# Attention statistics moved from VectorE to GpSimd, with a re-ranked order of issue and a second output tile

## The chip, the core and the metric

The kernel runs on one core of a Trainium2 chip. TensorE (PE) multiplies matrices, VectorE (DVE), ScalarE (ACT) and GpSimd (POOL) work on tiles in SBUF, SyncE (SP) issues the transfers. Each engine takes its instructions in the order in which the program lists them and waits for the others by semaphores. The metric is the device time of one execution in microseconds (us), as the median of several runs.

## What is computed

The reference has three stages, each feeding the next. The inputs q and k are scaled by 8 in this case, so that the scores are far from zero and the maxima matter.

```python
q_pool = q.reshape(B, H, S // 2, 2, D).mean(axis=3)          # B 2, H 8, S 1152, D 64
scores = scale * np.matmul(q_pool, k.transpose(0, 1, 3, 2))
scores = scores - np.max(scores, axis=-1, keepdims=True)
attn = np.exp(scores)
attn = attn / (np.sum(attn, axis=-1, keepdims=True) + 1e-09)
x = np.matmul(attn, v)                                        # then (1152 tokens, 512)
out += p[:, e:e + 1] * (np.maximum(x @ w1[e], 0.0) @ w2[e])   # 4 experts, 1024 wide
y = elu(x @ w_in) @ w_out                                     # 2048 wide
```

## The kernel before

**Tiling.** There are 16 heads (2 batches of 8). Two heads make a pair; a pair has 1152 pooled queries, that is 9 blocks of 128 rows. The fifth block belongs half to the even head and half to the odd one. So there are 72 blocks, and 8 of them have the score matmuls of two heads. The 1152 keys of a block are cut in two parts, z = 0 (640 keys) and z = 1 (512 keys), each with a maximum and an exponential of its own.

**The steps of the attention, by their letters in the code.** S are the score matmuls of a block and part (`scores`, line 430). R is the negated maximum of the part on VectorE (`max_all`, line 450), E the exponential with its sum on ScalarE (`exp`, line 457). T transposes the exponentials, three 128x128 pieces at a time, into one of two PSUM banks (line 493); D and G copy such a bank into `pt` on VectorE or ScalarE (`evac`, line 500). V multiplies `pt` with v (`values`, line 513, two halves h), O copies the result from the same two banks into `xo` (line 539). Because the two parts were scaled by different maxima, each half of a head's result has to be multiplied by a factor. These factors come from the **statistics** of the head, tiles named `st` of 128 x 5 x 2 or 128 x 4 x 2 numbers: `st00`/`st10` hold the negated maxima of both parts, `st01`/`st11` the sums, `st02`/`st12` the factors. I (`greater`, line 473) takes the smaller negated maximum and the two differences, J (line 479) their exponentials on ScalarE, K (`factors`, line 483) the weighted sum, its reciprocal and the two factors. Steps 3 and 4 send the factors through DRAM and back, broadcast, as the tile `fb`. X (`x_scaled`, line 556, GpSimd) multiplies `xo` with `fb` and adds the two halves, H and L (lines 561 and 564) split the result in a high and a low part `XH`, `XL` for the next stage.

**Preparation of a head.** a, b, c make Q (sum of neighbours, high part, low part), d and e make the high and low part of K (`k_high` line 411 on ScalarE, `k_low` line 415 on GpSimd in two halves). q, k and v are the loads.

**What sets the order.** `order_of` (line 159) is a list scheduler that runs while the program is built. It has a table `STAGES` (line 27) with a cost for each step on each engine that may take it, and a rank offset; of the steps that could start first it takes the one of the lowest rank (block number plus offset). What it writes is the order on every engine's queue and, for D, G and O, the engine. Nothing is reordered on the chip.

**After the attention** come 12 groups of two weight matrices (`first` line 698, `second` line 720), three matmuls for each product with high and low parts (`product`, line 680). GpSimd makes the low part of the weights (`conv_low`, line 304).

Of the kernel before, what the change touches and what calls it, by code (L numbers as in the profile page):

```python
# [10 lines left out]
F32 = mybir.dt.float32  # L11
# [14 lines left out]

STAGES = {
    "S": (dict(PE=585), 8),
    "R": (dict(DVE=822), 1.5),
    "E": (dict(ACT=920), 4),  # L30
    "I": (dict(DVE=330), 2),
    "J": (dict(ACT=250), 1.5),
    "K": (dict(DVE=720), -8),
    "3": (dict(SP=500), 2),
    "4": (dict(SP=500), 2),
    "X": (dict(POOL=4240), 0),
    "T": (dict(PE=327), 2),
    "D": (dict(ACT=480, DVE=557), -4),
    "G": (dict(ACT=480, DVE=557), 0),
    "V": (dict(PE=2620), 6),  # L40
    "O": (dict(ACT=720, DVE=750), 0),
    "H": (dict(ACT=690), 8),
    "L": (dict(POOL=1414), 1),
    "a": (dict(POOL=1400), 5),
    "b": (dict(ACT=686), -2),
    "c": (dict(DVE=1400), 0.5),
    "d": (dict(ACT=1160), -3),
    "e": (dict(POOL=1450), 5),
    "q": (dict(SP=1900), -9),
    "k": (dict(SP=1900), -9),  # L50
# [22 lines left out]
MB = 9  # L73
# [6 lines left out]
def blocks_of(i):  # L80

    return range(MB * (i // 2) + 4 * (i % 2), MB * (i // 2) + 5 + 4 * (i % 2))


def attention_ops(NH, KC):

    ops = {}

    def op(rank, before, x, *k, after=0):
        ops[(x, *k)] = [b for b in before if b], rank + STAGES[x][1], after  # L90

    NB = NH // 2 * MB
    U = range(3)
    
    t = 2700
    for i in range(NH):
        b = blocks_of(i)[0]
        zs = range(2) if i < 2 else range(1)
        if i > 1:
            old = [(x, i - 2, z) for x in "be" for z in range(2) if (x, i - 2, z) in ops]  # L100
            old += [("c", i - 2, z) for z in range(2) if ("c", i - 2, z) in ops]
            op(b, old, "q", i)
            op(b, old, "k", i)
        op(b, [("V", i - 3, 1)] if i > 2 else [], "v", i, after=9000)

        free = [("S", x, z) for x in blocks_of(i - 4) for z in (0, 1)] if i > 3 else []
        for z in zs:
            t += 1700 if i < 2 else 0
            op(b, [i > 1 and ("q", i)], "a", i, z, after=t if i < 2 else 0)
            op(b, [("a", i, z), *free], "b", i, z)  # L110
            op(b, [("b", i, z)], "c", i, z)
            op(b, [i > 1 and ("k", i), *free], "d", i, z, after=t if i < 2 else 0)
        for z in range(2):
            op(b, [("d", i, z % len(zs))], "e", i, z)
    for b in range(NB):
        p, m = divmod(b, MB)

        hs = [2 * p] * (m < 5) + [2 * p + 1] * (m > 3)
        need = [(x, i, z) for x in "ce" for i in hs for z in range(2) if (x, i, z) in ops]
        if b < 2:  # L120
            need.remove(("c", 0, 1))
        for z in (0, 1):
            op(b + 0.3 * z, need, "S", b, z)
            op(b + 0.3 * z, [("S", b, z)], "R", b, z)
            op(b + 0.3 * z, [("R", b, z), *[("T", b - NP, u) for u in U if b >= NP]], "E", b, z)
        for u in U:
            op(b, [("E", b, z) for z in (0, 1) if (z == 0 and 3 * u < CUT) or (z and 3 * u + 3 > CUT)] + [("V", i - 2, 1) for i in hs if i > 1], "T", b, u)
            op(b, [("T", b, u)], "D", b, u)
            if m == 4:
                op(b, [("T", b, u)], "G", b, u)  # L130
        if m in (4, 8):
            i = hs[0]
            for h in (0, 1):
                cs = range(CUT, KC) if h else range(CUT)
                ds = [("D", x, u) for x in blocks_of(i) for u in sorted({c // 3 for c in cs})]
                if i % 2:
                    ds = [("G", *x[1:]) if x[1] == blocks_of(i)[0] else x for x in ds]
                op(b + 0.5 * h, ds + [("V", i, 0) if h else ("v", i)], "V", i, h)
                op(b + 0.5 * h, [("V", i, h)] + [("L", i - 2)] * (i > 1), "O", i, h)
            op(b, [("E", b, 0), ("E", b, 1)], "I", i)  # L140
            op(b, [("I", i)], "J", i)
            op(b, [("J", i)], "K", i)
            op(b, [("K", i), i > 1 and ("4", i - 2)], "3", i)
            op(b, [("3", i), i % 2 and ("3", i - 1), i > 1 and ("X", i - 2)], "4", i)
            op(b, [("O", i, 0), ("O", i, 1), ("4", i)], "X", i)
            op(b, [("X", i)], "H", i)
            op(b, [("H", i)], "L", i)
    op(0, [], "p", after=40000)
    w = NB - 30
    for j in range(8):  # L150
        op(w + j, [("S", w + j, 0)], "w", j)
# [78 lines left out]
def attention_then_moe_then_elu_ffn(  # L230
# [32 lines left out]
    XH = const.tile([P, DC, T], F32R, name="XH")  # L263
    XL = const.tile([P, DC, T], F32R, name="XL")
# [4 lines left out]
    def f(ap):  # L269
        return ap.bitcast(F32)  # L270
# [45 lines left out]
    with ExitStack() as actx:  # L316
# [4 lines left out]
        mx_p = actx.enter_context(tc.tile_pool(name="mx", bufs=1))  # L321
        x_p = actx.enter_context(tc.tile_pool(name="xp", bufs=1))
# [6 lines left out]
        HQ = Q // 2  # L329
# [48 lines left out]
        def half(z):  # L378
            return slice(z * HQ, z * HQ + HQ)
# [89 lines left out]
        def stats(i):  # L469
            c = slice(MH + 1, MB) if i % 2 else slice(0, MH + 1)  # L470
            return [t[:, c] for t in st[i // 2 % 2]]

        def greater(e, i):
            m, _, t = stats(i)
            tt("DVE", t[:, :, 0], m[:, :, 0], m[:, :, 1], ALU.min)
            tt("DVE", t[:, :, 1], t[:, :, 0], m[:, :, 1], ALU.subtract)
            tt("DVE", t[:, :, 0], t[:, :, 0], m[:, :, 0], ALU.subtract)

        def factors_exp(e, i):
            t = stats(i)[2]  # L480
            nc.scalar.activation(t, t, AF.Exp)

        def factors(e, i):
            m, s, t = stats(i)
            tt("DVE", s, s, t, ALU.mult)
            nc.vector.scalar_tensor_tensor(
                out=s[:, :, 0], in0=s[:, :, 0], scalar=1e-9, in1=s[:, :, 1], op0=ALU.add, op1=ALU.add
            )
            nc.vector.reciprocal(out=s[:, :, 0], in_=s[:, :, 0])
            for z in (0, 1):  # L490
                tt("DVE", t[:, :, z], t[:, :, z], s[:, :, 0], ALU.mult)

        def transposes(e, b, u, n):
            tb[b, u] = t = bank[n]
# [33 lines left out]
        def rows(i):  # L528
            return slice(D * (i % 2), D * (i % 2) + D)

        def x_part(i, t):
            b, h = heads[i]
            return t[rows(i), h // 2, b * Q : b * Q + Q]


        xo = x_p.tile([P, 2, Q], F32, name="xo")
        fb = x_p.tile([P, 2 * Q], F32, name="fb")

        def output(e, i, h):
            o = tb.pop((i, h))  # L540
            for z in (0, 1):
                copy(e, xo[rows(i), h, half(z)], o[D * z : D * z + D, :HQ])

        def factors_out(e, i):
            p, y = divmod(i, 2)
# [8 lines left out]
            nc.sync.dma_start(out=fb[rows(i)], in_=d.unsqueeze(0).to_broadcast([D, 2 * Q]))  # L554

        def x_scaled(e, i):
            x = xo[rows(i)]
            tt(e, x, x, fb[rows(i)].rearrange("p (q z) -> p z q", z=2), ALU.mult)
            tt(e, x[:, 0], x[:, 0], x[:, 1], ALU.add)

        def x_high(e, i):
            copy(e, x_part(i, XH), xo[rows(i), 0])

        def x_low(e, i):
            tt(e, x_part(i, XL), xo[rows(i), 0], f(x_part(i, XH)), ALU.subtract)

        def norm_probs(e):
            r = mx_p.tile([P, TC, E], F32, tag="pn", name="pn", bufs=1)
# [11 lines left out]
            nc.sync.dma_start(out=pr.rearrange("e (p c) -> p e c", p=P), in_=r)  # L580

        do = dict(
            S=scores, R=max_all, E=exp, I=greater, J=factors_exp, K=factors, X=x_scaled, T=transposes, V=values, O=output,
            H=x_high, L=x_low, q=load_q, k=load_k, v=load_v, a=q_sum, b=q_high, c=q_low,
            d=k_high, e=k_low, p=norm_probs, y=lambda e: load_w(1), w=lambda e, j: wops[j](),
            g=lambda e, j: conv_high(e, 0, j, w_e), f=lambda e, j: conv_low(e, 0, j),
            G=lambda e, b, u: evac(e, b, u, 1),
            D=lambda e, b, u: evac(e, b, u, 0 if b % MB == MH else None),
# [250 lines left out]
```

## Time and profile before

| | us |
|---|---|
| median of 3 runs | 910.0 (909.78 to 911.85) |
| the profiled execution | 911.97 |
| its span, first to last instruction | 910.3 |
| of it, up to the end of the last V | 304.8 |

The profile page gives the busy time of each engine, its share of the span, the costliest groups of instructions with what ended the idle time before them, and the chain of waits that ended last, followed back from the last instruction. PE is busy 95% of the span, VectorE 58%, ScalarE 40% and GpSimd 49%. These shares mix two stages that look different: the attention, where all four engines work on each other's results, and the two products behind it, where PE has no gap.

### The profile page before, as it was taken

The page shows a single profiled execution, that of the slowest core. Times are in us where ns is not written, and L with a number is a line of the kernel's source. Part 1 is how long each engine was busy: PE and PEld are TensorE (multiplying, and loading weights), DVE is VectorE, ACT ScalarE, POOL GpSimd, SP SyncE. Part 2 cuts the span into 40 slices and gives each one's busy share as a digit, 9 for nine tenths or more (in the row PEclk, how much of TensorE's full clock was granted, in tenths as well). Part 3 has the DMA queues.
Part 4 walks back from the last instruction along what each step waited for, and adds up shares of the span by engine and source line. Part 5 has one row for each costly group of instructions (what it writes and reads, how often), then busy time and mean ns, then how long its engine had stood idle before and what let it go on. Part 6 is the DMA issues. An engine that isn't in the chain of part 4 may idle for free.

```text
span 910.3 us, 13830 instructions
## 1 busy us (share of the span) xinstructions
PE 865.5 (95%) x5374; PEld 797.8 (88%) x5374; DVE 530.1 (58%) x820; ACT 366.6 (40%) x746; POOL 443.6 (49%) x298
## 2 busy tenths in 40 slices
PE   8898899787998999999999999999999999999998
PEld 7565667666676799999999999999999999999998
DVE  7897978878677145556465565465565632333333
ACT  5786867666676422221221221312213253313221
POOL 3366655564613632546555454546464472624321
PEclk9999999897999999999999999999999999999999
DMA  7466253651220243513343324324144211000011
GB/s 236 80 144 143 68 144 67 151 143 27 86 40 10 57 185 105 166 46 123 109 142 102 130 82 129 130 62 168 36 130 148 101 62 47 1 1 2 1 40 66
DMA packets 40353, 84.37 MB, mean 93 GB/s; under 512 B 14304, under 2 KB 17376, under 8 KB 37344
## 3 DMA queue, kind: packets, MB, share of 16 engines
q1 hardware_dynamic: 40288, 83.49, 32.1%
q8 instruction: 42, 0.69, 0.3%
q14 instruction: 23, 0.19, 0.1%
HBM read 72.63 MB, written 10.84 MB: 92 GB/s over the span
## 4 chain that ended last, share of the span: by engine, by line
PE 79%; DVE 11%; issue 3%; ACT 2%; POOL 2%; DMA 1%; SPq 0%; DVEq 0%; ACTq 0%; POOLq 0%
PE p L684 60%; PE t L519 8%; PE s L442 6%; PE t L496 5%; DVE st L278 4%; DVE st L453 3%; DVE pt L275 2%; POOL acc L739 1%; ACT e L459 1%; ACT pt L275 1%; DMA k<-in 1%; POOL l L278 1%; DVE xo L275 1%; POOL xo L278 0%; DVE nt L643 0%
## 5 line engine op out<-in xcount | busy, mean ns | idle before, releaser
L684 PE MATMUL p<-XH,h 128*128 128x384 f32 (+1 forms) x608 | 198.6, 327 | 2.4 <-DVE hl L706 2.0
L684 PE MATMUL p<-XL,h 128*128 128x384 f32 (+1 forms) x608 | 198.3, 326 | 0.0
L684 PE MATMUL p<-hh,l 128*128 128x384 f32 (+1 forms) x608 | 198.0, 326 | 0.2 <-POOL l L278 0.2
L684 PE MATMUL p<-XH,l 128*128 128x384 f32 (+1 forms) x608 | 198.2, 326 | 0.0
L684 PE MATMUL p<-hl,h 128*128 128x384 f32 (+1 forms) x608 | 197.9, 326 | 0.0
L684 PE MATMUL p<-hh,h 128*128 128x384 f32 (+1 forms) x608 | 197.9, 326 | 0.0
L278 POOL TENSOR_TENSOR l<-w,h 128x512 fp32r<-128x512 f32 x96 | 125.6, 1326 | 70.9 <-ACT h L275 70.8
L705 ACT ACTIVATE hh<-p 128x768 fp32r<-128x768 f32 (+1 forms) x50 | 39.4, 789 | 278.0 <-PE p L684 277.9
L706 DVE SCALAR_TENSOR_TENSOR hl<-p,hh 128x768 fp32r<-128x768 f32 (+1 forms) x50 | 46.3, 926 | 162.3 <-ACT hh L705 162.3
L496 PE MATMUL t<-ident,e 128*128 128x128 f32 x648 | 106.1, 289 | 32.4 <-DVE pt L275 24.3
L496 PEld LDWEIGHTS t<-ident,e 128*128 128x128 f32 x648 | 79.5, 146 | 59.1 <-DVE pt L275 31.6
L442 PE MATMUL s<-K,Q 128*128 128x320 f32 (+1 forms) x480 | 120.2, 372 | 4.2 <-DVE K L278 2.3
L684 PEld LDWEIGHTS p<-XH,h 128*128 128x128 f32 x608 | 114.1, 188 | 2.9 <-DVE hl L706 2.2
L684 PEld LDWEIGHTS p<-XL,h 128*128 128x128 f32 x608 | 114.1, 188 | 0.4 <-issue 0.4
L684 PEld LDWEIGHTS p<-hh,l 128*128 128x128 f32 x608 | 114.1, 188 | 0.4 <-POOL l L278 0.4
L684 PEld LDWEIGHTS p<-hh,h 128*128 128x128 f32 x608 | 114.1, 188 | 0.0
L684 PEld LDWEIGHTS p<-hl,h 128*128 128x128 f32 x608 | 114.1, 188 | 0.0
L684 PEld LDWEIGHTS p<-XH,l 128*128 128x128 f32 x608 | 114.1, 188 | 0.0
L453 DVE TENSOR_REDUCE st<-s 128x1 f32<-128x640 f32 (+1 forms) x144 | 104.9, 749 | 8.7 <-PE s L442 7.7
L459 ACT ACTIVATE e<-s,st 128x640 f32<-128x640 f32 (+1 forms) x144 | 106.4, 747 | 7.9 <-DVE st L453 7.5
L658 POOL TENSOR_TENSOR nt<-nt,ne 128x512 f32<-128x512 f32 x32 | 41.8, 1307 | 121.8 <-issue 61.5
L718 POOL TENSOR_TENSOR hl<-e,hh 128x768 fp32r<-128x768 f32 (+1 forms) x26 | 44.8, 1723 | 110.2 <-ACT hh L717 110.1
(57 smaller groups left out, 1107.2 us busy)
## 6 DMA issues: line engine op xcount, KB each, us to landing
w<-in_wb SPq DMA_DIRECT2D x8, 1024.0 KB, 6.6
d<-in_va SPq DMA_DIRECT2D x16, 512.0 KB, 4.8
w<-nt SPq DMA_DIRECT2D x32, 256.0 KB, 3.3
d<-in_vb SPq DMA_DIRECT2D x16, 512.0 KB, 4.5
w<-w SPq DMA_DIRECT2D x8, 1024.0 KB, 6.5
q<-in_q SPq DMA_DIRECT2D x56, 144.0 KB, 3.0
k<-in_k SPq DMA_DIRECT2D x56, 144.0 KB, 3.5
w<-in_wa SPq DMA_DIRECT2D x7, 1024.0 KB, 6.4
```

The costliest lines, as they stand in the source:

```text
L275: (nc.scalar.copy if e == "ACT" else engines[e].tensor_copy)(out, a)
L278: engines[e].tensor_tensor(out=out, in0=a, in1=b, op=op)
L442: nc.tensor.matmul(out=t[:, j], lhsT=q[:, x, o : o + P], rhs=ks[p % 2][:, y, c : c + PARTS[z][1]], start=k == x == 0, stop=2 * k + x == last,)
L453: nc.vector.tensor_reduce(out=nm[b, z], in_=s_t[b, z], axis=AX.XY, op=ALU.max, negate=True)
L459: nc.scalar.activation(et[b % NP][:, part(z)].rearrange("p (j k) -> p j k", j=PARTS[z][0]), s_t.pop((b, z)), AF.Exp, bias=nm.pop((b, z)), ...
L496: nc.tensor.transpose(t[:, c * P : c * P + P], et[b % NP][:, (3 * u + c) * P : (3 * u + c + 1) * P], ident)
L519: nc.tensor.matmul(out=tb[i, h][64 * z : 64 * z + 64, :HQ], lhsT=raws[i, "v"][:, c, :], rhs=pt[i % 2][:, c, half(z)], start=c == cs[0], st ...
L658: nc.gpsimd.tensor_tensor(out=t, in0=t, in1=e, op=ALU.add)
L684: nc.tensor.matmul(out=ps, lhsT=w[:, c, m * P : m * P + P], rhs=x[:, c], start=c == 0 and w is hi and x is xh, stop=c == 3 and w is lo,)
L705: nc.scalar.activation(oh, s, AF.Relu)
L706: nc.vector.scalar_tensor_tensor(out=ol, in0=s, scalar=0.0, in1=f(oh), op0=ALU.max, op1=ALU.subtract)
L718: nc.gpsimd.tensor_tensor(out=ol, in0=e, in1=f(oh), op=ALU.subtract)
```

## The change

**Statistics.** Before, I was three VectorE instructions and K five. Now I is one `tensor_reduce` (minimum over the pair of maxima) on VectorE. The two differences are a step U on GpSimd, the weighted sum with its small constant (now a tile `eps`) is K with three instructions on GpSimd, the reciprocal is a step M on VectorE, and the two last products are a step N on GpSimd. So for each of the 16 heads VectorE has 2 small instructions where it had 8, and GpSimd has 7 more. The chain of a head was VectorE, ScalarE, VectorE; now it is VectorE, GpSimd, ScalarE, GpSimd, VectorE, GpSimd.

**Output tile.** `xo` becomes two tiles that take turns by pair, and O waits for L of four heads earlier instead of two.

**Ranks.** The table's costs and rank offsets change, so the whole order of the attention is written anew.

```diff
-    "R": (dict(DVE=822), 1.5),
+    "R": (dict(DVE=822), 8),
-    "I": (dict(DVE=330), 2),
+    "I": (dict(DVE=220), 1.2),
+    "U": (dict(POOL=400), 1.2),
-    "K": (dict(DVE=720), -8),
+    "K": (dict(POOL=600), 1.2),
+    "M": (dict(DVE=200), 1.2),
+    "N": (dict(POOL=400), 1.2),
...
-    "d": (dict(ACT=1160), -3),
+    "d": (dict(ACT=1160), 1.5),
...
-                op(b + 0.5 * h, [("V", i, h)] + [("L", i - 2)] * (i > 1), "O", i, h)
+                op(b + 0.5 * h, [("V", i, h)] + [("L", i - 4)] * (i > 3), "O", i, h)
...
         def greater(e, i):
             m, _, t = stats(i)
-            tt("DVE", t[:, :, 0], m[:, :, 0], m[:, :, 1], ALU.min)
-            tt("DVE", t[:, :, 1], t[:, :, 0], m[:, :, 1], ALU.subtract)
-            tt("DVE", t[:, :, 0], t[:, :, 0], m[:, :, 0], ALU.subtract)
+            nc.vector.tensor_reduce(out=t[:, :, 0], in_=m, axis=AX.X, op=ALU.min)
+
+        def differences(e, i):
+            m, _, t = stats(i)
+            for z in (1, 0):
+                tt(e, t[:, :, z], t[:, :, 0], m[:, :, z], ALU.subtract)
...
+        def whole_sum(e, i):
+            _, s, t = stats(i)
+            tt(e, s, s, t, ALU.mult)
+            tt(e, s[:, :, 0], s[:, :, 0], s[:, :, 1], ALU.add)
+            tt(e, s[:, :, 0], s[:, :, 0], eps[:, : s.shape[1]], ALU.add)
+
+        def recip(e, i):
+            s = stats(i)[1][:, :, 0]
+            nc.vector.reciprocal(out=s, in_=s)
+
         def factors(e, i):
-            m, s, t = stats(i)
-            tt("DVE", s, s, t, ALU.mult)
-            nc.vector.scalar_tensor_tensor(
-                out=s[:, :, 0], in0=s[:, :, 0], scalar=1e-9, in1=s[:, :, 1], op0=ALU.add, op1=ALU.add
-            )
-            nc.vector.reciprocal(out=s[:, :, 0], in_=s[:, :, 0])
+            _, s, t = stats(i)
             for z in (0, 1):
-                tt("DVE", t[:, :, z], t[:, :, z], s[:, :, 0], ALU.mult)
+                tt(e, t[:, :, z], t[:, :, z], s[:, :, 0], ALU.mult)
...
-        xo = x_p.tile([P, 2, Q], F32, name="xo")
+        xos = [x_p.tile([P, 2, Q], F32, name="xo%d" % j) for j in range(2)]
```

**VectorE, statistics of head 14.** In these rows `st_117` are the negated maxima, `st_118` the sums, `st_119` the factors, `s_` the scores in PSUM, `t_` a bank of transposes, `x2` means two alike in a row. Before:

```order
L278 TENSOR_TENSOR st_119<-st_117 128x5
L278 TENSOR_TENSOR st_119<-st_119,st_117 128x5 x2
L275 COPY pt_102<-t_105 128x3x128
L453 TENSOR_REDUCE st_117<-s_108 128x1
L278 TENSOR_TENSOR st_118<-st_118,st_119 128x10
L486 SCALAR_TENSOR_TENSOR st_118<-st_118 128x5
L489 RECIPROCAL st_118<-st_118 128x5
L278 TENSOR_TENSOR st_119<-st_119,st_118 128x5 x2
L275 COPY pt_102<-t_105 128x3x128
```

After, for the same head on the same engine:

```order
L484 TENSOR_REDUCE st_119<-st_117 128x5
L462 TENSOR_REDUCE st_117<-s_108 128x1
L281 COPY pt_102<-t_105 128x3x128
L462 TENSOR_REDUCE st_117<-s_107 128x1
L462 TENSOR_REDUCE st_117<-s_109 128x1
L281 COPY pt_102<-t_104 128x3x128
L503 RECIPROCAL st_118<-st_118 128x5
```

Of the eight statistics instructions two stay, each with one SBUF operand, and the reciprocal stands some rows further from the minimum.

**GpSimd, the two low halves of K of head 7.** `K_113` is K of the odd pairs, `xo` and `XL` are the steps X and L. Before:

```order
L278 TENSOR_TENSOR q<-q 128x2x288
L278 TENSOR_TENSOR xo<-xo,fb 64x1152
L278 TENSOR_TENSOR xo<-xo 64x576
L278 TENSOR_TENSOR K_113<-k,K_113 64x576
L278 TENSOR_TENSOR XL<-xo,XH 64x576
L278 TENSOR_TENSOR K_113<-k,K_113 64x576
```

After, for the same head (`st_114` to `st_116` are the statistics of head 5):

```order
L284 TENSOR_TENSOR st_116<-st_116,st_114 128x4 x2
L284 TENSOR_TENSOR xo_123<-xo_123,fb 64x1152
L284 TENSOR_TENSOR xo_123<-xo_123 64x576
L284 TENSOR_TENSOR st_115<-st_115,st_116 128x8
L284 TENSOR_TENSOR st_115<-st_115 128x4
L284 TENSOR_TENSOR st_115<-st_115,eps 128x4
L284 TENSOR_TENSOR K_113<-k,K_113 64x576
L284 TENSOR_TENSOR XL<-xo_123,XH 64x576
L284 TENSOR_TENSOR st_116<-st_116,st_115 128x4 x2
L284 TENSOR_TENSOR K_113<-k,K_113 64x576
```

The statistics of head 5 now stand ahead of these two halves, and between them. In the order that the planner writes, 14 score groups (S of one block and part) stood between the last low half of K of head 7 and the first score group that reads it; now there is none. For the odd heads 3 to 15 this distance was 8 to 18 groups and is now 0 to 2.

**PE, the end of the attention.** `pt_102` holds the transposes of even heads, `pt_103` those of odd heads; `x10` and `x8` are the halves h = 0 and h = 1 of V. Before:

```order
L519 MATMUL t_105<-pt_102,v 64x288 x10
L496 MATMUL t_104<-ident,e_98 128x128 x3
L684 MATMUL p_2762<-XH,h 128x288
L684 MATMUL p_2762<-XL,h 128x288
L684 MATMUL p_2762<-XH,l 128x288
L684 MATMUL p_2762<-XH,h 128x288
L496 MATMUL t_105<-ident,e_98 128x128 x3
L519 MATMUL t_104<-pt_102,v 64x288 x8
L519 MATMUL t_105<-pt_103,v 64x288 x10
L519 MATMUL t_104<-pt_103,v 64x288 x8
```

After:

```order
L704 MATMUL p_2781<-XH,l 128x288
L513 MATMUL t_104<-ident,e_98 128x128 x3
L536 MATMUL t_105<-pt_102,v 64x288 x10
L536 MATMUL t_104<-pt_103,v 64x288 x10
L536 MATMUL t_105<-pt_102,v 64x288 x8
L536 MATMUL t_104<-pt_103,v 64x288 x8
```

The second half of head 14 now comes behind the first half of head 15, so one half of V stands between it and the end where two stood.

## Rows read from the trace of the kernel before

**Rows 1.** The page's chain that ended last, by engine and by line.

```profile
PE 79%; DVE 11%; issue 3%; ACT 2%; POOL 2%; DMA 1%; SPq 0%; DVEq 0%; ACTq 0%; POOLq 0%
```

**Rows 2.** Stretches: length, busy us of PE, PEld, DVE, ACT, POOL, clock, DMA, GB/s.

```profile
9.00:300.00 291.00, 255.81 (x1680) 191.52 (x1682) 234.17 (x445) 206.34 (x500) 147.87 (x92) 0.94 0.43 98
325.00:350.00 25.00, 25.00 (x191) 25.00 (x190) 13.96 (x20) 7.87 (x14) 13.05 (x10) 1.00 0.36 133
```

**Rows 3.** The statistics on VectorE, by tile st: count, ns minimum/median/maximum, first and last start.

```profile
L278 DVE TENSOR_TENSOR st<-st,st x80: 150/166/5127, 23.7 to 290.5; 128x5 f32<-128x5 f32 x32, 128x4 f32<-128x4 f32 x32, 128x10 f32<-128x10 f32 x8, 128x8 f32<-128x8 f32 x8
...
L489 DVE RECIPROCAL st<-st x16: 179/186/192, 27.9 to 290.2; 128x5 f32<-128x5 f32 x8, 128x4 f32<-128x4 f32 x8
```

**Rows 4.** Groups by line, 0 to 400 us: busy us, mean ns, idle before.

```profile
L278 DVE TENSOR_TENSOR st<-st,st 128x5 f32<-128x5 f32 (+2 forms) x80 | 36.1, 469 | 1.9 <-ACT st L481 0.3
L278 DVE TENSOR_TENSOR st<-st 128x5 f32<-128x5 f32 (+1 forms) x16 | 8.7, 545 | 0.0
L486 DVE SCALAR_TENSOR_TENSOR st<-st 128x5 f32<-128x5 f32 (+1 forms) x16 | 5.1, 318 | 0.6
L489 DVE RECIPROCAL st<-st 128x5 f32<-128x5 f32 (+1 forms) x16 | 3.0, 186 | 0.5
L407 DVE SCALAR_TENSOR_TENSOR Q<-q,Q 128x576 fp32r<-128x576 f32 (+1 forms) x18 | 17.7, 984 | 1.8 <-issue 1.8
```

**Rows 5.** Timeline of 195 to 212 us: start, duration, what [idle before <-releaser].

```profile
199.14 2.52 POOL L278 TENSOR_TENSOR l<-w,h 128x512 fp32r<-128x512 f32 x2
...
200.49 6.48 DVE L278 TENSOR_TENSOR st<-st,st 128x5 f32<-128x5 f32 x2
...
205.53 1.41 POOL L278 TENSOR_TENSOR q<-q 128x576 f32<-128x576 f32 x1
...
207.49 0.90 PE L496 MATMUL t<-ident,e 128*128 128x128 f32 x3 [6.49 <-DVE pt L275]
```

**Rows 6.** Timeline of PE: the first and the last of ten gaps over 1.4 us.

```profile
29.73 0.70 PE L496 MATMUL t<-ident,e 128*128 128x128 f32 x3 [2.77 <-DVE pt L275]
...
290.16 0.55 PE L496 MATMUL t<-ident,e 128*128 128x128 f32 x3 [1.63 <-ACT pt L275]
```

**Rows 7.** The chain in order of time: start, us, what.

```profile
30.43 4.08 PE t L519 x20
...
146.65 2.58 PE t L519 x20
```

**Rows 8.** Stretches as in rows 2, around the two pieces of rows 7.

```profile
29.00:36.00 7.00, 6.27 (x34) 3.75 (x35) 3.42 (x8) 4.34 (x9) 3.11 (x3) 0.76 0.46 80
146.00:153.00 7.00, 7.00 (x52) 5.07 (x52) 4.68 (x11) 6.45 (x15) 1.08 (x1) 1.00 0.41 46
```

**Rows 9.** GpSimd's groups by shape, 0 to 320 us.

```profile
L278 POOL TENSOR_TENSOR K<-k,K 64x576 fp32r<-64x576 f32 x30 | 42.9, 1445 | 61.1 <-ACT K L275 50.2 <-DMA k<-in_k 6.2 <-issue 3.6
L278 POOL TENSOR_TENSOR q<-q 128x288 f32<-128x288 f32 x4 | 3.5, 878 | 5.5 <-DMA q<-in 5.5
L828 POOL MEMSET const-uint8-127<- 128x1 uint8 x1 | 0.1, 102 | 0.0
```

**Rows 10.** PE's score matmuls by shape, 134 to 161 us.

```profile
L442 PE MATMUL s<-K,Q 128*128 128x320 f32 x35 | 7.1, 328 | 0.0
L442 PE MATMUL s<-K,Q 128*128 128x512 f32 x18 | 6.0, 426 | 0.2 <-ACT e L459 0.2
```

**Rows 11.** Waits before 360 us: engine, line, waited for, us, times, longest.

```profile
POOL K L278 <- ACT K L275: 50.2, 7, 10.4
...
ACT st L481 <- DVE st L278: 19.7, 11, 6.1
```

**Rows 12.** Timeline at the attention's end: last V, GpSimd's weights, PE's wait for them.

```profile
298.29 6.53 PE L519 MATMUL t<-pt,v 128*64 128x288 f32 x52
...
314.42 5.04 POOL L278 TENSOR_TENSOR l<-w,h 128x512 fp32r<-128x512 f32 x4
...
319.51 0.40 PE L684 MATMUL p<-hh,l 128*128 128x288 f32 x1 [0.21 <-POOL l L278]
```

More of the change, by code (lines that the diff above doesn't have):

```diff
@@ L28 @@
     "S": (dict(PE=585), 8),
-    "R": (dict(DVE=822), 1.5),
+    "R": (dict(DVE=822), 8),
     "E": (dict(ACT=920), 4),
-    "I": (dict(DVE=330), 2),
+    "I": (dict(DVE=220), 1.2),
+    "U": (dict(POOL=400), 1.2),
     "J": (dict(ACT=250), 1.5),
-    "K": (dict(DVE=720), -8),
+    "K": (dict(POOL=600), 1.2),
+    "M": (dict(DVE=200), 1.2),
+    "N": (dict(POOL=400), 1.2),
     "3": (dict(SP=500), 2),
     "4": (dict(SP=500), 2),
-    "X": (dict(POOL=4240), 0),
+    "X": (dict(POOL=4240), 6),
     "T": (dict(PE=327), 2),
-    "D": (dict(ACT=480, DVE=557), -4),
-    "G": (dict(ACT=480, DVE=557), 0),
+    "D": (dict(ACT=480, DVE=557), -3),
+    "G": (dict(ACT=480, DVE=557), -4),
     "V": (dict(PE=2620), 6),
@@ L42 @@
     "H": (dict(ACT=690), 8),
-    "L": (dict(POOL=1414), 1),
+    "L": (dict(POOL=1414), 3),
     "a": (dict(POOL=1400), 5),
-    "b": (dict(ACT=686), -2),
-    "c": (dict(DVE=1400), 0.5),
-    "d": (dict(ACT=1160), -3),
+    "b": (dict(ACT=686), 1),
+    "c": (dict(DVE=1100), 4),
+    "d": (dict(ACT=1160), 1.5),
     "e": (dict(POOL=1450), 5),
@@ L138, in attention_ops @@
                 op(b + 0.5 * h, ds + [("V", i, 0) if h else ("v", i)], "V", i, h)
-                op(b + 0.5 * h, [("V", i, h)] + [("L", i - 2)] * (i > 1), "O", i, h)
+                op(b + 0.5 * h, [("V", i, h)] + [("L", i - 4)] * (i > 3), "O", i, h)
             op(b, [("E", b, 0), ("E", b, 1)], "I", i)
-            op(b, [("I", i)], "J", i)
+            op(b, [("I", i)], "U", i)
+            op(b, [("U", i)], "J", i)
             op(b, [("J", i)], "K", i)
-            op(b, [("K", i), i > 1 and ("4", i - 2)], "3", i)
+            op(b, [("K", i)], "M", i)
+            op(b, [("M", i)], "N", i)
+            op(b, [("N", i), i > 1 and ("4", i - 2)], "3", i)
             op(b, [("3", i), i % 2 and ("3", i - 1), i > 1 and ("X", i - 2)], "4", i)
@@ L424, in attention_then_moe_then_elu_ffn @@
         st = [[mx_p.tile([P, MB, 2], F32, name="st%d%d" % (j, x), bufs=1) for x in range(3)] for j in range(2)]
+        eps = mx_p.tile([P, MB], F32, name="eps")
+        nc.vector.memset(eps, 1e-9)
         def part(z):
@@ L533, in x_part, with xo @@
             return t[rows(i), h // 2, b * Q : b * Q + Q]
-        xo = x_p.tile([P, 2, Q], F32, name="xo")
+        xos = [x_p.tile([P, 2, Q], F32, name="xo%d" % j) for j in range(2)]
         fb = x_p.tile([P, 2 * Q], F32, name="fb")
+        def xo(i):
+            return xos[i // 2 % 2][rows(i)]
         def output(e, i, h):
@@ L541, in output @@
             for z in (0, 1):
-                copy(e, xo[rows(i), h, half(z)], o[D * z : D * z + D, :HQ])
+                copy(e, xo(i)[:, h, half(z)], o[D * z : D * z + D, :HQ])
         def factors_out(e, i):
@@ L556, in x_scaled @@
         def x_scaled(e, i):
-            x = xo[rows(i)]
+            x = xo(i)
             tt(e, x, x, fb[rows(i)].rearrange("p (q z) -> p z q", z=2), ALU.mult)
@@ L561, in x_high @@
         def x_high(e, i):
-            copy(e, x_part(i, XH), xo[rows(i), 0])
+            copy(e, x_part(i, XH), xo(i)[:, 0])
         def x_low(e, i):
-            tt(e, x_part(i, XL), xo[rows(i), 0], f(x_part(i, XH)), ALU.subtract)
+            tt(e, x_part(i, XL), xo(i)[:, 0], f(x_part(i, XH)), ALU.subtract)
         def norm_probs(e):
@@ L582, in attention_then_moe_then_elu_ffn @@
         do = dict(
-            S=scores, R=max_all, E=exp, I=greater, J=factors_exp, K=factors, X=x_scaled, T=transposes, V=values, O=output,
+            S=scores, R=max_all, E=exp, I=greater, U=differences, J=factors_exp, K=whole_sum, M=recip, N=factors, X=x_scaled, T=transposes, V=values, O=output,
             H=x_high, L=x_low, q=load_q, k=load_k, v=load_v, a=q_sum, b=q_high, c=q_low,
```

## The prediction

> **What bounds the kernel now.** I read the chain first [rows 1]: PE holds 79% of it and VectorE 11%, so nearly all of the time is matmuls, and what can be won lies where PE waits for VectorE. The stretches [rows 2] say where that is. From 325 us on PE is busy 25.00 of 25.00 us; the weights' stage is PE's alone, and nothing that the change touches stands there. From 9 to 300 us PE is busy 255.8 of 291 us, VectorE 234.2, ScalarE 206.3, GpSimd 147.9, and the granted clock is 0.94. So 35 us of PE are idle in the attention, and no engine is full there.
>
> Next I asked what VectorE does in its 234 us. The small statistics stand out [rows 3]: an instruction on 5 numbers per partition takes 166 ns in the median, but up to 5127 ns. The reciprocal, of the same size, never leaves 179 to 192 ns. The timeline shows what separates them [rows 5]: the two differences start at 200.49 and end at 206.97, while GpSimd runs one tensor operation behind another, from 199.14 until 206.94. The slow instructions read two tiles of SBUF, the reciprocal one: a two-operand instruction of VectorE waits until GpSimd's queue has a break. Behind it in VectorE's queue stands the copy that frees a transpose bank, and PE, which has two banks, is idle for 6.49 us.
>
> **What the change takes from VectorE.** The four groups of a head's eight instructions are busy 36.1 + 8.7 + 5.1 + 3.0 = 52.9 us [rows 4]. At their undisturbed length they would be 112 x 0.166 + 16 x 0.186 = 21.6 us [rows 3], so 31.3 us are waiting for GpSimd. Afterwards 16 minima and 16 reciprocals are left, all with one SBUF operand. The reciprocal's row prices both: 32 x 0.186 = 6.0 us. The minimum is not in these rows in this form. Were it slowed like the others it would be 0.469 us [rows 4] and 4.5 us dearer in all; I take 0.186, the nearest in kind. VectorE loses about 47 us.
>
> **Where the waiting was on the path.** Ten gaps of PE of more than 1.4 us follow right behind a stretched statistic: 2.77, 1.48, 2.26, 1.81, 2.00, 3.39, 6.49, 2.06, 1.93 and 1.63 us, from 29.73 to 290.16 us [rows 5, 6]. Their sum is **25.8 us**. That is the first term, -25.8. The rest of the 31.3 us was hidden by banks and blocks already in work, and I count nothing for it.
>
> **The clock.** After several of these gaps the clock is at its lower level of 1.2 GHz for a while. The same 20 matmuls of V take 4.08 us behind the gap at 29.73 and 2.58 us elsewhere [rows 7]; the granted clock of 29 to 36 us is 0.76, of 146 to 153 us it is 1.00 [rows 8]. 0.24 of 7 us lost at half speed is 3.4 us at the lower level, and it cost 1.5 us. Over the attention 0.06 of 291 us are lost, 35 us at the lower level, that is ten such pieces: 15 us if all go, nothing if they stay. Some lie at the start or where PE waits anyway, so I take half: **-8 us**.
>
> **What GpSimd gets.** 16 x 7 = 112 instructions of 4 to 10 numbers per partition. No row has their size. The two bounds are a memset at 0.10 us and the sum of q on 288 columns at 0.88 us [rows 9]: 11 to 99 us in all. From 576 to 288 columns the price falls from 1.45 to 0.88 us; that line ends near 0.3 us at no columns, and I take 0.3, an estimate: 34 us. GpSimd has 143 of 291 us free, so the load is no bound, but its queue is in order. Three new waits stand on it or on others: J on ScalarE waits for U, with exponentials and copies behind it; M on VectorE waits for K, with maxima and copies behind it; K and N on GpSimd wait for these, with the low half of K behind them. ScalarE waited for J before too, 19.7 us in 11 waits [rows 11], mostly for the same stretched instructions. The place where it can hurt is the low half of K of the odd heads. It moves from 8 to 18 score groups ahead of its use to 0 to 2, seven times (heads 3 to 15), and five statistics instructions of the odd head before, 1.5 us at 0.3, stand ahead of it. On PE the two V groups ahead of that use, 18 pairs of matmuls or 36 x 0.126 = 4.5 us by the row of the last V [rows 12], cover it in part. Bounds: nothing, and 7 x 7.2 = 50 us if GpSimd is held as long as its mean wait for ScalarE's half now [rows 11]. Nearest is the added work itself; half of 1.5 us seven times is **+5 us**.
>
> The Trainium skill, "GPSIMD Engine Reference", section "Engine selection", speaks against the move: elementwise work of two inputs belongs on VectorE, GpSimd being about twice as slow. By that rule alone 112 x 2 x 0.166 = 37 us of work would replace 21.6. The rows show the other side: what VectorE really spends on these instructions is 52.9 us, since most of it is waiting.
>
> **The rest.** The second `xo` tile lets O of a head run without waiting for L of two heads before; no gap of PE named above ends with such a wait, so it brings nothing. At the end, V of head 14 ends one half later against the end of V: 16 matmuls, 2.0 us. X and L of head 14, then of head 15, then four weight halves follow on GpSimd without a break until 319.46 us, and PE waits for the last of them for 0.21 us [rows 12]. PE's work there is used up exactly, so these 2.0 us land: **+2 us**. The factors of the last head go through three more hops; before them lie the last blocks and V, some 10 us of PE, and I count nothing. Had GpSimd's queue no room there, each 0.3 us of it would land in full.
>
> **The sum.** The profiled execution took 911.97 us, with a span of 910.3. 911.97 - 25.8 - 8 + 2 + 5 = 885.2 us. The median of the runs is 2.0 us below the profiled one, so I predict **883 us**, 3% less.
>
> **Rivals.** *More than the gaps.* Between 134 and 161 us no statistic is stretched; PE does 53 score matmuls, six to a block, that is 8.8 blocks or 3.06 us for one [rows 10]. The attention has 72 blocks, 8 of them double: at that pace 80 x 3.06 = 245 us instead of 291, 46 us less, 864 us. For it: ScalarE would be at 84% and PE below full. Against it: the order is new, and a stretch behind a stall may profit from what was kept back.
>
> *The low half of K comes too late (slower).* GpSimd sits in its in-order queue at K or N of a head, waiting for ScalarE or VectorE, while PE waits for the K half behind it. Without this term the change gains 25.8 + 8 - 2 = 31.8 us, so it turns at 31.8 / 7 = 4.5 us for each odd head. At the 7.2 us of rows 11 the time is 911.97 - 31.8 + 50 - 2.0 = 928 us. For it: the margin of 0 groups, and three changes of engine ahead. Against it: GpSimd is free for half of the stretch, and V lies in front.
>
> *The stall only changes its place (no change).* Eighteen instructions on VectorE still read two SBUF tiles, the low half of Q, 17.7 us [rows 4], and GpSimd's queue becomes denser; new waits of J and M on ScalarE and VectorE take back what the statistics gave, 32 waits of about 1 us. Then the time is 908 to 912 us. The Trainium skill, "Perfetto Trace Analysis", section "Optimizing Scalar/DVE Operations", says this much: the two engines share a read port of SBUF, so moving work between them might not help. Against it stands the row of the reciprocal, which is not disturbed: what stays on VectorE is of its kind.
>
> *Half.* If half of the gaps close and the clock gains nothing: 911.97 - 13 + 2 + 5 - 2 = 904 us.
>
> **Chances.** The forecast, 870 to 897: 0.62. More than the gaps: 0.13. Half: 0.08. No change: 0.07. Slower: 0.10. About 0.3%, 2.7 us, is what a measurement of this kernel can tell from no change. That makes faster 0.83, same 0.07, slower 0.10. The range of 863 to 903 takes in the forecast and most of its two neighbours; it leaves out the cases at 908 and above.
>
> **What would show it.** In the profile of the changed kernel: the minimum and the reciprocal at about 0.19 us without long ones; the ten gaps of PE gone, and the granted clock of the attention at 0.97 or above; small `st` instructions on GpSimd of about 0.3 us; the last V ending near 277 us. The forecast is wrong where score matmuls wait for the low half of K, or for ScalarE at J, by more than a few us in all, or where GpSimd's small instructions take 0.8 us.

## The result, and the profile after

The changed kernel takes **874.25 us** (median of 4 runs, 872.45 to 874.62) where the kernel before took 910.16 in the same comparison. The ratio is 0.9598, with a 95% interval of 0.9580 to 0.9616. That is 36 us less; 27 were forecast, and 874 lies inside the range of 863 to 903. The profiled execution took 874.62 us with a span of 872.8, against 911.97 and 910.3 before: 37.5 us of span.

The first view is the chain that ended last, by engine, as in [rows 1].

```profile
PE 85%; DVE 6%; ACT 3%; issue 2%; POOL 2%; DMA 1%; SPq 0%; DVEq 0%; ACTq 0%
```

VectorE's part has fallen from 11% to 6%, and PE's has risen. Where the time went is read from two stretches, from 9 us to the end of the last V in each kernel. The columns are those of [rows 2]: length, busy us of PE, PEld, DVE, ACT, POOL, granted clock, DMA. The kernel before, whose last V ends at 304.8 us [rows 12]:

```profile
9.00:305.00 296.00, 260.81 (x1720) 194.37 (x1721) 234.17 (x445) 208.05 (x505) 151.42 (x94) 0.94 0.42 97
```

The changed kernel, and two stretches at its end:

```profile
9.00:264.00 255.00, 244.50 (x1716) 183.31 (x1714) 190.17 (x344) 207.18 (x510) 170.87 (x204) 1.00 0.49 112
260.00:275.00 15.00, 12.19 (x93) 9.80 (x89) 0.76 (x1) 4.83 (x10) 10.04 (x6) 1.00 0.08 21
275.00:300.00 25.00, 23.98 (x170) 23.98 (x171) 9.91 (x13) 8.02 (x15) 12.65 (x10) 0.93 0.52 192
```

Two things changed in nearly the same number of PE instructions. PE was idle 296 - 260.8 = 35.2 us and is idle 255 - 244.5 = 10.5 us: 24.7 us. And PE's busy time fell from 260.8 to 244.5 us, by 16.3 us, for the same work: the granted clock was 0.94 and is 1.00. (0.06 x 296 = 17.8 us of clock came back in all; a part of the lower clock had lain in PE's gaps, where it cost nothing.) The two make up the 41.0 us by which the stretch is shorter; the last V ends at 264.2 instead of 304.8, 40.6 us earlier. From there to the end of the span it is 608.6 us where it was 605.5, so 3.1 us are given back at the end of the attention.

The statistics themselves, by tile `st` (count, ns minimum/median/maximum, first and last start), answer to [rows 3]:

```profile
L284 POOL TENSOR_TENSOR st<-st,st x80: 194/203/723, 24.9 to 257.0; 128x5 f32<-128x5 f32 x32, 128x4 f32<-128x4 f32 x32, 128x10 f32<-128x10 f32 x8, 128x8 f32<-128x8 f32 x8
L484 DVE TENSOR_REDUCE st<-st x16: 146/152/156, 24.6 to 248.8; 128x5 f32<-128x10 f32 x8, 128x4 f32<-128x8 f32 x8
...
L284 POOL TENSOR_TENSOR st<-st x16: 195/201/590, 27.0 to 256.1; 128x5 f32<-128x5 f32 x8, 128x4 f32<-128x4 f32 x8
L284 POOL TENSOR_TENSOR st<-st,eps x16: 196/198/204, 27.7 to 256.3; 128x5 f32<-128x5 f32 x8, 128x4 f32<-128x4 f32 x8
L503 DVE RECIPROCAL st<-st x16: 163/179/183, 28.1 to 256.6; 128x5 f32<-128x5 f32 x8, 128x4 f32<-128x4 f32 x8
```

On VectorE the longest is now 183 ns, where it was 5127. On GpSimd an instruction of this size takes 0.20 us.

What PE waited for most from 9 to 300 us in the kernel before, and what it still waits for (engine, line, waited for, us, times, longest):

```profile
PE t L496 <- DVE pt L275: 24.3, 15, 6.5
```

```profile
PE p L704 <- DVE hl L726: 3.8, 2, 3.0
PE t L513 <- DVE pt L281: 3.5, 6, 1.2
PE t L513 <- ACT e L468: 1.8, 2, 1.1
PE t L513 <- ACT pt L281: 1.8, 5, 0.4
PE t L536 <- DVE pt L281: 1.1, 3, 0.5
PE t L513 <- DVE xo L281: 0.8, 2, 0.6
PE s L451 <- ACT e L468: 0.2, 1, 0.2
```

The transposes wait 3.5 us for VectorE's copies where they waited 24.3, with no wait over 1.2. No row has a score matmul waiting for K. The largest wait is that of the first matmuls of the weights' stage: two waits, 3.8 us in all, where the kernel before had one of 2.0 us, behind 300 us.

### The profile page after: what moved, and what is told of

It reads as the page before. It is cut to its first block, busy times and chain, and to the rows that moved or that the text cites. A ratio compares the mean times of both kernels' runs of the same rounds, so it can differ in the third digit from the quotient of the medians.

```text
span 872.8 us, 13895 instructions
## 1 busy us (share of the span) xinstructions
PE 851.9 (98%) x5374; PEld 789.3 (90%) x5374; DVE 486.5 (56%) x720; ACT 365.8 (42%) x752; POOL 466.4 (53%) x409
## 4 chain that ended last, share of the span: by engine, by line
PE 85%; DVE 6%; ACT 3%; issue 2%; POOL 2%; DMA 1%; SPq 0%; DVEq 0%; ACTq 0%
PE p L704 63%; PE t L536 8%; PE s L451 7%; PE t L513 6%; DVE st L462 2%; DVE pt L281 1%; POOL xo L284 1%; ACT pt L281 1%; POOL acc L759 1%; ACT e L468 1%; DVE xo L281 1%; DMA k<-in 1%; DVE Q L413 1%; DVE nt L663 0%; ACT XH L281 0%
## 5 line engine op out<-in xcount | busy, mean ns | idle before, releaser
L451 PE MATMUL s<-K,Q 128*128 128x320 f32 (+1 forms) x480 | 115.8, 361 | 2.3 <-DVE K L284 1.6
L513 PE MATMUL t<-ident,e 128*128 128x128 f32 x648 | 100.0, 278 | 8.4 <-DVE pt L281 3.5
L513 PEld LDWEIGHTS t<-ident,e 128*128 128x128 f32 x648 | 75.3, 140 | 33.8 <-DVE pt L281 7.7
```

Of the source, the lines that this page charges most:

```text
L451: nc.tensor.matmul(out=t[:, j], lhsT=q[:, x, o : o + P], rhs=ks[p % 2][:, y, c : c + PARTS[z][1]], start=k == x == 0, stop=2 * k + x == last,)
L513: nc.tensor.transpose(t[:, c * P : c * P + P], et[b % NP][:, (3 * u + c) * P : (3 * u + c + 1) * P], ident)
```

## The experiments

The theory is the prediction's: a VectorE instruction with two operands in SBUF stands still while GpSimd's queue runs, PE's banks are not freed in this time, and the clock falls behind the longer gaps. The rivals are that the new order of issue did it, that it is VectorE's load (the number of its instructions), or the second output tile. Each result is a median of 4 runs, and its ratio is to the kernel before on the same chip. They ran on three chips: the kernel before took 910.73 us beside e1 to e4, 912.73 beside e5 to e7 and 912.91 beside e8 and e9, against 910.16 beside the changed kernel. So where a difference to the changed kernel is only a few us, the one that follows from the two ratios is given too.

### The statistics alone, in the old order (e1)

```diff
-    "I": (dict(DVE=330), 2),
+    "I": (dict(DVE=220), 2),
+    "U": (dict(POOL=400), 2),
...
-    "K": (dict(DVE=720), -8),
+    "K": (dict(POOL=600), -8),
+    "M": (dict(DVE=200), -8),
+    "N": (dict(POOL=400), -8),
```

The functions and their dependencies are those of the change; everything else is the kernel before.

> The kernel before with the statistics' new engines alone (steps U, K, N on GpSimd, I and M on VectorE); the old ranks and one xo tile stay. If the two-operand waits of VectorE are the cause, most of the 36 us come back here: 876 to 888 us, with the ten gaps of PE (25.8 us) gone and the clock of the attention at 0.98 or more. If the new order of issue is the cause, under 10 us: 900 to 908 us.

Measured: 876.24 us, ratio 0.9618 (0.9593 to 0.9642), 34.5 us less. The move alone brings all but 2 us of the change, and the intervals of the two ratios overlap. The stretch from 9 us to just behind its last V has the clock at 0.99:

```profile
9.00:269.00 260.00, 248.54 (x1716) 185.15 (x1715) 186.69 (x339) 208.01 (x514) 173.38 (x206) 0.99 0.49 110
```

Its last V ends at 269.1 us, 4.9 us later than in the changed kernel (in part by a piece at 1.2 GHz at the start, which that kernel does not have), and from there to the end it is 605.4 us, 3.3 us less. So in these two profiles the new order shortens the attention and gives most of that back behind it.

### The order and the second tile alone (e2)

```diff
-    "I": (dict(DVE=220), 1.2),
-    "U": (dict(POOL=400), 1.2),
+    "I": (dict(DVE=330), 1.2),
...
-    "K": (dict(POOL=600), 1.2),
-    "M": (dict(DVE=200), 1.2),
-    "N": (dict(POOL=400), 1.2),
+    "K": (dict(DVE=720), 1.2),
```

Against the changed kernel; the functions are those of before.

> The changed kernel with all statistics back on VectorE as three and five instructions (steps I, J, K); the new ranks and two xo tiles stay. If the two-operand waits are the cause, it lies near the kernel before, 895 to 912 us, with statistics of up to several us on VectorE. If the order is the cause, 878 to 888 us.

Measured: 897.5 us, ratio 0.9845 (0.9813 to 0.9876), 13 us less than before. So the order does something by itself, at the end of the first theory's range that was nearest to the rival. Its statistics show a part of the reason (tile `st`, as above; the profile is of the slowest of the four runs, 901.04 us):

```profile
L278 DVE TENSOR_TENSOR st<-st,st x80: 152/166/2599, 24.9 to 276.6; 128x5 f32<-128x5 f32 x32, 128x4 f32<-128x4 f32 x32, 128x10 f32<-128x10 f32 x8, 128x8 f32<-128x8 f32 x8
L278 DVE TENSOR_TENSOR st<-st x16: 151/170/3794, 24.7 to 270.0; 128x5 f32<-128x5 f32 x8, 128x4 f32<-128x4 f32 x8
```

```profile
9.00:291.00 282.00, 256.55 (x1721) 191.63 (x1723) 224.85 (x425) 212.59 (x526) 146.24 (x92) 0.96 0.46 102
```

The waiting is still there, but less of it: the four groups are busy 28.9 + 10.3 + 5.0 + 3.0 = 47.2 us, 25.6 us above their undisturbed length where it was 31.3, and the longest is 3.8 us instead of 5.1. PE is idle 25.5 us instead of 35.2, and the clock is 0.96 instead of 0.94. PE's idle time fell by more than the waiting did; what in the order hides the rest was not tried. The two parts, 34.5 and 13 us, do not add up to 36, which fits: with the statistics gone from VectorE, the order has little left to avoid.

### The same order and number, one operand each (e3)

```diff
-            tt("DVE", t[:, :, 0], m[:, :, 0], m[:, :, 1], ALU.min)
-            tt("DVE", t[:, :, 1], t[:, :, 0], m[:, :, 1], ALU.subtract)
-            tt("DVE", t[:, :, 0], t[:, :, 0], m[:, :, 0], ALU.subtract)
+            nc.vector.reciprocal(out=t[:, :, 0], in_=m[:, :, 1])
+            nc.vector.reciprocal(out=t[:, :, 1], in_=m[:, :, 1])
+            nc.vector.reciprocal(out=t[:, :, 0], in_=m[:, :, 0])
...
```

The five instructions of K likewise become reciprocals.

> The kernel before with its own order, where each of the eight statistics instructions is a reciprocal of the same size, with one SBUF operand; the factors are wrong by this. Nothing moves to GpSimd and VectorE has as many instructions. If it is the second operand that waits for GpSimd, they all take 0.18 to 0.2 us, the ten gaps go, and the time is 874 to 888 us. If it is the number of instructions or the load of VectorE, the time stays within 5 us of 910.

Measured: 871.42 us, ratio 0.9561 (0.9534 to 0.9587). This is the run that decides. VectorE's queue has the kernel before's order and as many instructions, nothing is added to GpSimd, and 39 us are gone, more than in the change and 2.6 us more than the expected range allowed. By line (busy us, mean ns, idle before):

```profile
L485 DVE RECIPROCAL st<-st 128x10 f32<-128x10 f32 (+1 forms) x16 | 3.2, 200 | 0.0
L487 DVE RECIPROCAL st<-st 128x5 f32<-128x5 f32 (+1 forms) x16 | 3.0, 186 | 0.5
```

```profile
9.00:263.00 254.00, 245.25 (x1719) 184.77 (x1718) 203.02 (x445) 205.41 (x504) 151.57 (x94) 1.00 0.49 112
```

VectorE is busy 203 us, 13 more than in the changed kernel, and PE is idle 8.8 us. Neither the number of instructions nor the order had to change; what cost the 39 us was the second SBUF operand.

The Trainium skill, "SBUF — State Buffer", section "Who interferes with whom", says that a VectorE instruction with two SBUF inputs and a GpSimd instruction that reads SBUF exclude each other, and that a reduction never does. The trace agrees: in the kernel before, 27 of the 112 two-operand statistics took over 0.4 us, and each of the 27 ended 0.02 to 0.03 us behind the end of a GpSimd instruction, while the changed kernel's 16 minima, reductions, all took 0.146 to 0.156 us. Which end it was can be read from two stretches of the kernel before (timeline, start and duration):

```profile
201.61 1.41 POOL L278 TENSOR_TENSOR XL<-xo,XH 64x576 fp32r<-64x576 f32 x1
202.96 1.41 POOL L278 TENSOR_TENSOR q<-q 128x576 f32<-128x576 f32 x1
204.31 1.27 POOL L278 TENSOR_TENSOR l<-w,h 128x512 fp32r<-128x512 f32 x1
...
218.97 1.41 POOL L278 TENSOR_TENSOR xo<-xo 64x576 f32<-64x576 f32 x1
219.06 2.72 DVE L278 TENSOR_TENSOR st<-st,st 128x4 f32<-128x4 f32 x2
220.34 1.41 POOL L278 TENSOR_TENSOR K<-k,K 64x576 fp32r<-64x576 f32 x1
221.70 1.41 POOL L278 TENSOR_TENSOR XL<-xo,XH 64x576 fp32r<-64x576 f32 x1
```

The two statistics that start at 219.06 end one with each GpSimd instruction, though the next GpSimd instruction follows at once. So it was with 24 of the 27. Three let ends pass: two of them one, and the longest, which started at 200.49 [rows 5] and took 5.127 us, the ends at 201.66, 203.02 and 204.37. Why those three waited on is open.

### One output tile (e4)

```diff
-                op(b + 0.5 * h, [("V", i, h)] + [("L", i - 4)] * (i > 3), "O", i, h)
+                op(b + 0.5 * h, [("V", i, h)] + [("L", i - 2)] * (i > 1), "O", i, h)
...
-        xos = [x_p.tile([P, 2, Q], F32, name="xo%d" % j) for j in range(2)]
+        xos = [x_p.tile([P, 2, Q], F32, name="xo%d" % j) for j in range(1)]
```

> The changed kernel with one xo tile, O waiting for L of two heads before as it did. By the prediction the second tile brings nothing: 874 us, within 3 us. If it frees O's banks of PSUM sooner, 878 to 885 us, with PE waiting for xo.

Measured: 873.9 us, ratio 0.9591 (0.9567 to 0.9615), the changed kernel's time. The second tile brings nothing.

### A hold on VectorE without GpSimd, short and long (e5, e8)

```diff
             nc.vector.tensor_reduce(out=t[:, :, 0], in_=m, axis=AX.X, op=ALU.min)
+            nc.vector.tensor_reduce(
+                out=junk, in_=ident.unsqueeze(1).to_broadcast([P, 14, P]), axis=AX.X, op=ALU.max
+            )
```

The long one has 28 in place of 14, at every second head.

> The changed kernel with one more instruction on VectorE behind each head's minimum: a reduction over 14 x 128 numbers of a constant tile, one SBUF operand, its result unused. It should take about 2 us, 16 times, so that VectorE is held for some 31 us as by the waits of the kernel before, without GpSimd having a part in it. If the time lost before was VectorE being held at this place (PE gaps, then the lower clock), 895 to 912 us, with gaps of 1 to 3 us behind the holds and ten or more pieces at 1.2 GHz. If the loss needs GpSimd's work at the same time, or the order now hides a hold, 876 to 885 us.

> The changed kernel with a hold on VectorE of twice the length of e5_hold's, about 4 us, behind the minimum of every second head: eight holds, again 32 us in all, one SBUF operand, result unused. If only the held time counts, 897 us as with the sixteen short holds. If long gaps of PE also bring its clock down, as in the kernel before, each hold costs a gap of some 3 us and a piece at 1.2 GHz: 902 to 914 us, with about eight such pieces.

Measured: 896.58 us for sixteen short holds, ratio 0.9833 (0.9808 to 0.9858), and 906.36 us for eight long ones, 0.9931 (0.9914 to 0.9948). The holds by line, the stretch to the last V or nearly so, the last V (start, duration), and PE's largest wait, for the short ones:

```profile
L486 DVE TENSOR_REDUCE junk<-ident 128x14 f32<-128x1792 f32 x16 | 32.1, 2009 | 0.0
```

```profile
9.00:285.00 276.00, 248.77 (x1726) 184.16 (x1726) 216.97 (x360) 208.26 (x511) 169.97 (x203) 1.00 0.46 103
...
275.98 8.95 PE L540 MATMUL t<-pt,v 128*64 128x288 f32 x72
...
PE t L517 <- DVE pt L281: 15.8, 16, 1.5
```

And for the long ones:

```profile
L487 DVE TENSOR_REDUCE junk<-ident 128x28 f32<-128x3584 f32 x8 | 31.0, 3876 | 0.0
```

```profile
9.00:295.00 286.00, 253.48 (x1698) 188.39 (x1698) 218.43 (x352) 207.60 (x508) 169.27 (x203) 0.96 0.44 99
...
288.57 8.95 PE L541 MATMUL t<-pt,v 128*64 128x288 f32 x72
...
PE t L518 <- DVE pt L281: 22.2, 13, 3.2
```

VectorE is held for the same time, 32.1 and 31.0 us, near the 31.3 us of waiting in the kernel before. Sixteen times 2 us cost 22.3 us against the changed kernel, eight times 3.9 us cost 32.1 (by the ratios 21 and 30). The short holds leave gaps of PE up to 1.5 us and the clock at 1.00: the gaps came as expected, the ten pieces at 1.2 GHz did not. The long holds leave gaps up to 3.2 us and the clock at 0.96, in six pieces where about eight were expected. The last V comes 12.6 us later with them; PE's idle time to there is 286 - 253.5 = 32.5 us where the short ones have 276 - 248.8 = 27.2, so 5.3 us of the 12.6 are longer gaps, and the rest goes with the clock. So a hold of VectorE costs PE gaps and clock without GpSimd having a part in it, and here the same sum cost more in eight long holds than in sixteen short ones.

What makes the clock fall is not shown by this. Seven of the long run's gaps are of 2.76 to 3.16 us; behind four of them the clock fell, behind three it did not. One more piece at 1.2 GHz follows two gaps of only 1.3 and 1.2 us, and one lies from 9.6 to 13.0 us, ahead of the first hold.

### The low half of K, early again (e9)

```diff
-    "d": (dict(ACT=1160), 1.5),
+    "d": (dict(ACT=1160), -3),
```

> The changed kernel with the old rank offset of step d (-3 in place of 1.5), so that the low half of K of the odd heads again comes 9 to 17 score groups ahead of its use. If its lateness costs what the prediction put on it, 5 us, the time is 868 to 871 us. If it costs nothing, 872 to 877 us.

Measured: 874.45 us, ratio 0.9581 (0.9565 to 0.9597), the changed kernel's time. But the equal time is a sum of two parts, as its last V shows:

```profile
261.09 6.53 PE L536 MATMUL t<-pt,v 128*64 128x288 f32 x52
```

It ends at 267.6 us, 3.4 us later than in the changed kernel, and what follows is shorter by as much, since the gaps at the end are smaller (the largest 1.15 us instead of 2.99) and no piece at the lower clock follows them. So this run alone does not price the lateness. That no score matmul of the changed kernel waits for K from 9 us on does: it costs PE nothing directly, and bringing K forward did not shorten the attention.

### The last two-operand instructions (e7)

```diff
-            engines[e].scalar_tensor_tensor(
-                out=q[:, 1], in0=a, scalar=SCALE, in1=f(q)[:, 0], op0=ALU.mult, op1=ALU.subtract
-            )
+            nc.vector.tensor_reduce(out=q[:, 1], in_=a.unsqueeze(3), axis=AX.X, op=ALU.max)
```

> The changed kernel with the low part of Q made by a reduction over one element, which reads one SBUF operand instead of two; the low part is wrong by this. These 18 are the last two-operand instructions of VectorE in the attention, 20.2 us against some 13 without waiting. If their waits are on the path too, 866 to 871 us. If they are hidden, 872 to 876 us.

Measured: 870.82 us, ratio 0.9546 (0.9523 to 0.9570), 3.4 us below the change, 4.7 by the ratios. The line of the changed kernel, then of this run:

```profile
L413 DVE SCALAR_TENSOR_TENSOR Q<-q,Q 128x576 fp32r<-128x576 f32 (+1 forms) x18 | 20.2, 1122 | 1.4 <-ACT Q L405 1.3
```

```profile
L413 DVE TENSOR_REDUCE Q<-q 128x576 fp32r<-128x576 f32 (+1 forms) x18 | 12.2, 677 | 0.1
```

So 8 us of VectorE's time in the changed kernel were still waiting, and some 3 to 5 us of it were on the path.

### The end of the attention (e6)

In the changed kernel the last V, PE's next gaps and what they wait for stand like this (timeline, start and duration):

```profile
255.23 8.95 PE L536 MATMUL t<-pt,v 128*64 128x288 f32 x72
...
263.17 2.68 POOL L284 TENSOR_TENSOR xo<-xo,fb 64x1152 f32<-64x1152 f32 x1 [5.99 <-ACT xo L281]
269.57 0.40 PE L704 MATMUL p<-XH,h 128*128 128x288 f32 x1 [0.84 <-DVE hl L726]
...
273.83 0.67 ACT L281 CAST XH<-xo 64x576 fp32r<-64x576 f32 x1 [5.11 <-POOL xo L284]
...
275.21 0.76 DVE L726 SCALAR_TENSOR_TENSOR hl<-p,hh 128x576 fp32r<-128x576 f32 x1 [5.69 <-ACT hh L725]
276.02 0.40 PE L704 MATMUL p<-XH,h 128*128 128x288 f32 x1 [2.99 <-DVE hl L726]
276.06 5.00 POOL L284 TENSOR_TENSOR l<-w,h 128x512 fp32r<-128x512 f32 x4
```

Steps X and L of heads 14 and 15 keep GpSimd busy until 276 us. ScalarE, in its order, has step H of head 15 (`XH`) ahead of `hh`, VectorE needs `hh` for `hl`, and PE waits for `hl`. So X of head 15 on GpSimd holds all three. VectorE is busy 0.76 of 15 us from 260 on.

```diff
     def of(o):
+        if o[0] == "X" and o[1] >= 14:
+            return dict(DVE=2300)
```

> The changed kernel with step X of heads 14 and 15 on VectorE, which is idle at the attention's end, instead of GpSimd. If GpSimd's chain X, L, X, L there is what holds PE before the second products (gaps of 0.84 and 2.99 us, and the piece at 1.2 GHz behind them), 868 to 872 us. If PE waits for something else there, 874 us.

Measured: **867.91 us** (867.31 to 868.46), ratio 0.9517 (0.9497 to 0.9537), 6.3 us below the changed kernel, 7.4 by the ratios, the lowest time of all the runs and just below the expected range. Its X on VectorE, GpSimd's weights, and its stretch from 260 us:

```profile
262.83 1.35 DVE L286 TENSOR_TENSOR xo<-xo,fb 64x1152 f32<-64x1152 f32 x1 [6.40 <-ACT xo L283]
...
270.86 5.04 POOL L286 TENSOR_TENSOR l<-w,h 128x512 fp32r<-128x512 f32 x4
```

```profile
260.00:320.00 60.00, 60.00 (x444) 58.20 (x439) 28.47 (x40) 19.02 (x34) 21.71 (x17) 1.00 0.37 130
```

The weights start 5.2 us earlier, PE has no gap, and the clock stays at 1.00.

## Why the prediction was right, and where it was off

**The stretched statistics.** Right, and shown: e3 takes the second operand away and nothing else, and the kernel falls by 39 us to 871.42, past the changed kernel. One step of the reading was too general: that such an instruction waits until GpSimd's queue has a break. In 24 of 27 cases it waited only until the end of the GpSimd instruction then running; the row that the prediction read it from, of 5.127 us, is the longest of the three exceptions. The minimum, which I priced at the reciprocal's 0.186 us, takes 0.152.

**The gaps, -25.8 us.** PE's idle time from 9 us to the last V fell by 24.7 us. None of the ten gaps has a successor: PE's longest gap in this stretch of the changed kernel is 1.2 us.

**The clock, -8 us.** This is the mis-sized term. I worked out 15 us if all the pieces at 1.2 GHz go and took half, because some would lie at the start or where PE waits anyway. PE's busy time fell by 16.3 us, twice the term. The kernel before has nine pieces. One of them lies at the start and half of another in the longest gap, as two stretches of it show:

```profile
9.00:13.00 4.00, 4.00 (x15) 3.16 (x16) 4.00 (x7) 2.27 (x6) 3.02 (x4) 0.57 0.44 127
...
204.00:207.40 3.40, 0.00 (x0) 0.00 (x0) 3.37 (x4) 0.21 (x1) 2.94 (x3) 0.51 0.00 0
```

So the reason for taking half was real, but it covers 3.4 us of clock, not half of it. All pieces but the first come behind, or in, one of the ten gaps, and they are gone with the gaps. The first, at most 1.7 us, is no gain of the change: the changed kernel has 1.00 in that place, but the profiles of e1, e6, e7, e8 and e9 have such a piece there.

**GpSimd's small instructions.** I took 0.3 us, between 0.10 and 0.88; they take 0.20, about 23 us in all for 112 of them. The rule that the Trainium skill gives in "GPSIMD Engine Reference", section "Engine selection", that an elementwise operation of two inputs is about twice as slow on GpSimd, does not hold at this size: 0.20 against 0.166 us.

**The low half of K, +5 us.** Wrong: it is zero. No score matmul waits for K in the trace after from 9 us on. GpSimd stood at K or N of the statistics 1.5 us at most, which the two V groups on PE, 4.5 us by the prediction's own count, can cover; at U it stood up to 10.3 us, and no score matmul waited there either.

**The end, +2 us.** Measured +3.1: the gaps there grew from 2.2 to 3.8 us, and a piece at the lower clock came behind the larger one, 0.07 x 25 = 1.7 us. Steps X and L of the last heads on GpSimd were the cause, as named (e6), but the way to PE was another: not over the weights' low half at the end of GpSimd's work, but over H on ScalarE, `hh` and `hl`. The piece at the lower clock was not foreseen.

**The second output tile, nothing.** Right (e4).

With the measured sizes the sum is -24.7 - 16.3 + 3.1 = -37.9 us, against 37.5 us of span; the 0.4 us between them comes from cutting the stretches at whole us. The forecast's terms sum to -26.8 us. It fell short by some 11 us: 8 of the clock and 5 of the low half of K, less 1 each of the gaps and the end. For the same reason the last V ends at 264.2 us and not near 277.

**The rivals.** *More than the gaps* lay about as near as the forecast, on the other side: 864 and 883 us around the measured 874. PE now does 80 block equivalents in 255 us, 3.19 us for one, where this rival had 3.06. *The stall only changes its place* has a small true part: the low half of Q went from 17.7 to 20.2 us on VectorE, and e7 finds 3 to 5 us of its waiting on the path. The move alone gave 34.5 us (e1), since what moved was the kind of instruction that waits. The caution of the Trainium skill, "Perfetto Trace Analysis", section "Optimizing Scalar/DVE Operations", that moving work between these two engines might not help, did not come true here. *The low half of K* did not happen.

## What to carry to other kernels

Look at the maximum beside the median of small VectorE instructions: if one with two SBUF operands takes many times its median, look whether it ends together with a GpSimd instruction, and if so move it, or give it one operand. A stall of VectorE can cost PE a gap and, behind some gaps, clock as well; in this kernel eight long stalls cost more than sixteen short ones of the same sum. Where a stage ends in a chain on one engine, look which engine is idle there.

## What the runs showed of the hardware

A VectorE instruction of 0.17 us with two SBUF operands waited up to 5.1 us. Of 112, 27 took over 0.4 us; every one of these ended 0.02 to 0.03 us behind the end of a GpSimd instruction, 24 of them with the first that ended, three with a later one. With one operand, the same number of instructions in the same places took 0.15 to 0.20 us on average (e3). GpSimd's tensor instructions on 4 to 10 numbers per partition take 0.20 us, hardly more than VectorE's 0.15 to 0.19. Eight holds of VectorE of 3.9 us cost 32.1 us and sixteen of 2.0 us cost 22.3; of the 12.6 us by which the last V comes later, 5.3 are longer gaps of PE, the rest goes with the granted clock (0.96 against 1.00).
